# A planner that counts two more delays on early loads, and the issue order it was given anew

## Chip, core and metric

The kernel runs on one core of one Trainium2 chip. The metric is the device time of one execution in microseconds (us), lower is better. The kernel before takes 402.11 us, the median of 3 runs (401.63 to 402.58).

## What is computed

Eight batches (B=8) of eight heads (H=8), sequence S=576, head size D=64, 32 packing queries per head. Attention is done twice: the packing queries p attend to k and v, which gives 32 packed rows per head; then q attends to these packed rows, which serve as keys and as values. The heads side by side are x, the input of a gated convolution block.

```python
p_packed = softmax(p @ k.T / 8) @ v             # 32 rows per head
x        = softmax(q @ p_packed.T / 8) @ p_packed
h        = relu(x @ w_in)                       # 512 -> 1024
conv     = sum_k conv_w[k] * shift(h, k - 1)    # along the sequence
out      = (h * sigmoid(conv)) @ w_out          # 1024 -> 512
```

The weights w_in, conv_w and w_out arrive as 8-byte floats and are turned into 4-byte floats on the chip.

## The kernel before

Work is cut into 16 groups g of four heads (two groups per batch) and, behind them, 8 blocks j of 128 columns of the first product per batch and 36 tiles m of 128 rows of the second. Each group, batch and tile is a Python generator (a stream) whose steps name an engine, a duration, the events to wait for and the buffers to take.

Per group: k and q are loaded (L404, L415) and transposed, for the first four groups on PE (L444) with ScalarE copies behind (L450), later on VectorE (L427); p is scaled (L484) and transposed (L487); PE scores p against k (L460), VectorE takes the maximum (L515, `nm`), ScalarE the exponential (L519, `a`), PE transposes it (L547), ScalarE copies it (L550, `a1T`), PE multiplies by v (L557), ScalarE scales (L576, `pb`), PE transposes (L581), ScalarE copies (L584, `ppT`), PE scores against q (L460 again). Then VectorE does a softmax over the 32 packed rows (L591 to L615) with one ScalarE exponential inside (L601), and the result is split into a high and a low half (L619 `a2hi` on ScalarE, L621 `a2lo` on VectorE).

Per batch and half hf of the columns: PE multiplies the packed rows by w_in (L641), ScalarE and PE or VectorE split that (L656 `ghi`, L660, L664 `glo`). A block j of the first product is 12 matmuls at L705; ScalarE and VectorE apply relu, convolution and gate (L717, L721, L723, L727, L731, L733). The tiles of the second product are at L794; the last pairs use seven products in place of eight at L926. Weights are loaded in eight pieces (L305), narrowed by ScalarE (L275) and VectorE (L277, L282), and the w_out pieces are split with PE's help (L333, L338, L342).

What sets the order: a table of stream numbers, `ORDER`. `Flow.run` walks it, issues each stream's next step, and books the planned time of it with the costs of `Step` and `Flow`. So the order of instructions on each engine's queue comes from the table alone, and each engine works through its queue in that order. The planner's times have one effect on the program: while the first tile of the second product is not done, `fill` puts idle 128x128 matmuls (L251) in front of a PE step whose planned start leaves room, at 216 ns each. One such fill shows as two records in the profile.

All loads go through SyncE's queue (SP), with eight semaphores in turn: a ninth load waits until the first of the eight before it has landed. The planner's landing time of a load is the one before it in one chain of transfers plus its own duration.

Of the kernel before, what the change touches and what calls it, by code (L numbers as in the profile page):

```python
# [26 lines left out]
    "1a0u1n0m0u124f6e1n451l4d4e4f6e0u454f4d1a4h1c4e4e0u0u4f4g1b0y1k4d451b4i4f4f114j4i881n884k4i6e1g4h6f4j6e6e4i6f6e4k"
    "4h4k4i4j4i89161i121a4k4j4i6e1i6f6f121e1a4j4k4l891d126f6f6f6f4j4k4l1i6f1o4k6g121s4l1i4l6g4h124l8a4m1a4l6f1a1j4m1q"
    "191j1i1a6f4m4j121i6g1q8a1w6g6h6e4n6g4m6h1q204n1a1v6g1i6g4m1v4l1h6g4m1a4n124m121r1v4n6g6g236f8b1a6g4o121i4n1i4o4p"
    "6h6h4o4p4p1a236h124o8b4o6h4n1q6g4p1a6h6h6h4p6h4o1m4o1a1y4n234p4p1q1i6h1i1q4q282b1y4r6i1r1y6i1y1a1i6i126i6i1q1a2b"  # L30
    "4r6i12241a4q4q1z6i6j1a6i1a4r1i6i6i4s6i2b1p4s6j4s1q4t4u1q4s1i1y1i4t4s264t1t4t1q1z6k1y2g6j2c4u6j1y4u4s261i6j2j4u6j"
    "4s6k6j264u2j4v4t2j1q6j271i4u1u4v226i4u6j266j4t2e1x4w2k6j4t1i4v1q2e1i1q6k4w2e4v2a1i1q6h2f2e4v3p6k6k6k4w1y1i274x26"
    "6k1q6k6l1y4x6l216k6k6k2f4x1q6k4x2m1y4v50266m1q6l6l4w264v1q26262r2m6l2h4w6l2m2r506l4x2r6j6l4y4w2e1q2n2z4y4y2z1y1y"
    "2z374x1q296l2n2o6l6l6l4w4z4z1y1y4y4z516m4y6m6m6m6m6m1q4y6m6m504z4x4z514z4y524z256n6m526n536m52536n526n1y52535452"
    "536n54546n6n6n6n6n1y1y522w552m2e6o54556o1y266n2s51532u2e2u6n5a54376o6p5553556p1y552654546o3c305a1y6o6o6o6o372e2e"
    "6o6o2p1y6o265656566p6p266p6p532u556q6m26562u576p5556266p6p57566p3f576q56586p59266q6q576q6q58582d5957592m58583457"
    "58596q6q6q596o6q575859596r2e26322m5a6q6r26262e6s5b6r6r6r3226262m2e326s2m2m6r2i6p5b6r2e5c6r6r6q5b6r5c322e5d335c6r"
    "3f3f6s5c6s2v5c2u2e5c2v2e2e2e6s5e6t5c6t355f385d5d5d5d6s6s6s6s2l5f5f5e5e2e6s3a5e5d3a2m6s2m2u2m5k3a5f2m5d2u2q3b2u6t"
    "6u6u6t6r6t6t5f5e5k5f2m5g5f5e6t6t6t5k6t3g6t5h6u6u6u326u5h5h2t6s2m2m6u3a6v5h2m5h5e5h6u6u2x332u6u2m2e5h2y2e5i5j5g5g"
    "6t5i5g2m5i3i5j6v325i5j6u5l3i2u325l325i5j5j3b5g2u362m5i5i2m6v6v6v6v3a2u5j3i5g5j2u5g6v326v6v6v6v6v6w5m5m5l6w313i2u"  # L40
    "2u6x6x5n5n5o6w6w6w6w2u6w2u5n6w6w5o5m6u5m5o6w6w323j3a5m5o5o5n6x6x2u6x6x6y326x6x5n5o5o5m5n3i5m3a3a6x5n5p5p5q5p325q"
    "6x5r3d6y3e396x325p5p5q5q2u5q5p6y6y323a325p5r5r6y6y6y6y6y2u5s2u5q5q5t6y6z6x3j32325r5u325s6w32323a5t6z5r325t3i5s5t"
    "6y5r5v5s5t5s3i6z5s6z3i5r5s6z6z6z6z6z6z5t5u6y5t5u70706z3a3a5w5w703a707071828470705x5w3h5v715w5x70708070705y71715w"
    "83813a3a70715y5w855y5x5x7172835w5y725y5x713i717185715v715z5z72725z5z723a3a723i5z3a5z713i64725x73645y5z727272603i"
    "723i7386605x3i607473733a73723i6z615y607g60643i3i3a60607373733a6162747362627373636174637474747473623i636261636274"
    "3i6563613i63633i656162816175747466676587747466757j7h686666676766757575676867836675767575756766686775757j696a7k7k"
# [6 lines left out]
class Step:  # L53
# [131 lines left out]
def tile_packed_attention_conv_gate(  # L185
# [15 lines left out]
    HG = 4  # L201
# [307 lines left out]
    def attention(g):  # L509
# [44 lines left out]
        t = small()  # L554
# [514 lines left out]
```

## Time and profile before

| what | value |
|---|---|
| median of 3 runs | 402.11 us |
| profiled execution | 402.01 us, span 400.2 us, so 1.8 us lie outside the span |
| PE, VectorE, ScalarE busy | 392.2, 365.5, 284.1 us |
| PE clock granted | 1.00 of full speed in nearly every slice |
| DMA | 49.2 MB, 360 GB/s at 10 to 30 us |

PE is busy for 98% of the span, but some of this is the idle fills. VectorE is busy 91%, and idle in the main at the two ends. ScalarE is busy for 10.0 of 10 us in the stretches from 40 to 70 us and has room later. A row of the chain of waits gives a start, the time until the next piece begins, and what filled it.

### The profile page before, as it was taken

How to read it: one execution, taken by the hardware profiler on the slowest of the kernel's cores; microseconds unless marked ns; L12 is line 12 of the kernel's file. 1: busy time of each engine (PE TensorE's matmuls, PEld its weight loads, DVE VectorE, ACT ScalarE, POOL GpSimd, SP SyncE). 2: the span in 40 equal slices, each digit the busy share in tenths (PEclk: the TensorE clock that was granted, in tenths of full speed). 3: DMA queues.
4: the chain of work that ended last, by engine and by line, in shares of the span. 5: the costliest groups of instructions: out<-in, count | busy, mean ns of one | idle time of the engine just before them, and what ended most of it. 6: DMA issues, size and time to landing. Idle time of an engine off the chain costs nothing.

```text
span 400.2 us, 8463 instructions
## 1 busy us (share of the span) xinstructions
PE 392.2 (98%) x3393; PEld 318.8 (80%) x3393; DVE 365.5 (91%) x532; ACT 284.1 (71%) x497; POOL 1.6 (0%) x16
## 2 busy tenths in 40 slices
PE   7899999999999999999999999999999999999996
PEld 6668676778868877878869687878788787889996
DVE  0789999999999999999999999999999999999751
ACT  4989999977687588666765659738657678876440
POOL 1000000000000000000000000000000000000000
PEclk9999999999999999999999999999999999999999
DMA  8999999999858782966483539113600110001202
GB/s 304 357 361 267 276 264 163 128 156 146 121 94 112 122 196 68 156 88 153 79 153 79 97 100 157 48 51 97 122 2 27 52 41 19 23 2 52 78 28 79
DMA packets 140378, 49.19 MB, mean 123 GB/s; under 512 B 121244, under 2 KB 132788, under 8 KB 140340
## 3 DMA queue, kind: packets, MB, share of 16 engines
q1 hardware_dynamic: 140340, 48.67, 55.8%
q8 instruction: 26, 0.43, 0.5%
q14 instruction: 12, 0.10, 0.1%
HBM read 37.25 MB, written 9.44 MB: 117 GB/s over the span
## 4 chain that ended last, share of the span: by engine, by line
PE 84%; ACT 8%; DMA 5%; SPq 1%; issue 1%
PE fo L794 44%; PE big L705 23%; PE big L460 3%; PE big L641 3%; DMA q<-in_q_dram 3%; PE big L926 3%; DMA v<-in_v_dram 2%; PE sm L926 2%; PE sm L557 2%; ACT hgt L731 1%; ACT hgt L721 1%; PE big L547 1%; ACT hgt L275 1%; ACT glo L664 1%; SPq L404 1%; PE sm L794 1%
## 5 line engine op out<-in xcount | busy, mean ns | idle before, releaser
L794 PE MATMUL fo<-wo_hi,xhi 128*128 128x512 f32 x240 | 97.9, 408 | 0.0
L794 PE MATMUL fo<-wo_lo,xhi 128*128 128x512 f32 x240 | 94.8, 395 | 0.0
L794 PE MATMUL fo<-wo_hi,xlo 128*128 128x512 f32 x240 | 94.5, 394 | 0.0
L717 ACT ACTIVATE hbuf<-big 128x576 f32<-128x576 f32 x64 | 42.3, 668 | 30.1 <-PE big L705 29.5
L731 ACT ACTIVATE hgt<-hgt 128x576 f32<-128x576 f32 x64 | 43.9, 696 | 18.8 <-DVE hgt L727 18.6
L794 PEld LDWEIGHTS fo<-wo_hi,xhi 128*128 128x128 f32 x240 | 45.3, 189 | 13.3 <-issue 2.5
L705 PE MATMUL big<-a2hi,ghi 128*128 128x288 f32 x256 | 55.6, 298 | 0.1
L705 PE MATMUL big<-a2hi,glo 128*128 128x288 f32 x256 | 54.5, 294 | 0.0
L705 PE MATMUL big<-a2lo,ghi 128*128 128x288 f32 x256 | 54.3, 294 | 0.0
L794 PEld LDWEIGHTS fo<-wo_lo,xhi 128*128 128x128 f32 x240 | 45.1, 188 | 11.2
L723 DVE SCALAR_TENSOR_TENSOR hgt<-hbuf,cw,hgt 128x576 f32<-128x576 f32 x64 | 51.1, 802 | 2.5 <-ACT hgt L721 2.3
L794 PEld LDWEIGHTS fo<-wo_hi,xlo 128*128 128x128 f32 x240 | 45.1, 188 | 7.9
L727 DVE SCALAR_TENSOR_TENSOR hgt<-hbuf,cw,hgt 128x576 f32<-128x576 f32 x64 | 50.7, 803 | 0.4
L721 ACT ACTIVATE hgt<-hbuf,cw 128x576 f32<-128x576 f32 x64 | 50.3, 792 | 1.0
L733 DVE SCALAR_TENSOR_TENSOR hgt<-hgt,hbuf 128x576 f32<-128x576 f32 x64 | 47.1, 745 | 0.7 <-ACT hgt L731 0.4
L705 PEld LDWEIGHTS big<-a2hi,ghi 128*128 128x128 f32 x256 | 42.7, 188 | 5.1 <-ACT glo L664 1.0
L705 PEld LDWEIGHTS big<-a2lo,ghi 128*128 128x128 f32 x256 | 40.9, 188 | 0.0
L705 PEld LDWEIGHTS big<-a2hi,glo 128*128 128x128 f32 x256 | 40.9, 188 | 0.0
L747 DVE TENSOR_TENSOR xlo<-hgt,xhi 128x1024 fp32r<-128x1024 f32 (+1 forms) x36 | 35.8, 1002 | 0.0
L858 ACT COPY o<-fo 128x512 f32<-128x512 f32 (+1 forms) x32 | 18.5, 580 | 21.2 <-PE fo L794 19.6
L744 ACT CAST xhi<-hgt 128x1024 fp32r<-128x1024 f32 (+1 forms) x36 | 31.5, 881 | 2.2 <-DVE hgt L733 2.2
L515 DVE TENSOR_REDUCE nm<-big 128x1 f32<-128x576 f32 x16 | 11.9, 746 | 11.6 <-PE big L460 11.5
(191 smaller groups left out, 604.1 us busy)
## 6 DMA issues: line engine op xcount, KB each, us to landing
out_dram<-o SPq DMA_DIRECT2D x35, 256.0 KB, 3.3
v<-in_v_dram SPq DMA_DIRECT2D x16, 512.0 KB, 5.9
k<-in_k_dram SPq DMA_DIRECT2D x48, 144.0 KB, 4.2
q<-in_q_dram SPq DMA_DIRECT2D x48, 144.0 KB, 4.1
hgt<-in_moe_w_in_dram SPq DMA_DIRECT2D x3, 1024.0 KB, 11.2
hgt<-in_moe_w_out_dram SPq DMA_DIRECT2D x3, 1024.0 KB, 6.6
a1T<-stage SPq DMA_DIRECT2D x96, 20.0 KB, 1.8
hgt<-in_k_dram SPq DMA_DIRECT2D x2, 576.0 KB, 5.1
```

Of the source, the lines that this page charges most:

```text
L705: nc.tensor.matmul(out=t[:, hf, :SH], lhsT=w[:, gg, js], rhs=x[:, hf * SH : (hf + 1) * SH], start=n == 0, stop=n == 3 * NG - 1,)
L717: nc.scalar.activation(out=h[:, 1 : S + 1].rearrange("c (f s) -> c f s", f=2), in_=t[:, :, :SH], func=AF.Relu, scale=0.5)
L721: nc.scalar.activation(out=d, in_=h[:, 1 : S + 1], func=AF.Copy, scale=cw[:, NJ + j : NJ + j + 1])
L723: nc.vector.scalar_tensor_tensor(out=d, in0=h[:, 0:S], scalar=cw[:, j : j + 1], in1=d, op0=ALU.mult, op1=ALU.add)
L727: nc.vector.scalar_tensor_tensor(out=d, in0=h[:, 2 : S + 2], scalar=cw[:, 2 * NJ + j : 2 * NJ + j + 1], in1=d, op0=ALU.mult, op1=ALU.add)
L731: nc.scalar.activation(out=d, in_=d, func=AF.Tanh)
L733: nc.vector.scalar_tensor_tensor(out=d, in0=d, scalar=1.0, in1=h[:, 1 : S + 1], op0=ALU.add, op1=ALU.mult)
L744: nc.scalar.copy(out=hi[:, js, o], in_=src[:, js])
L747: nc.vector.tensor_tensor(out=lo[:, js, o], in0=src[:, js], in1=hi[:, js, o].bitcast(F32), op=ALU.subtract)
L794: nc.tensor.matmul(out=t[:, : fs.stop - fs.start], lhsT=x, rhs=w[:, c, fs], start=c + i == 0, stop=c == NJ - 1 and i == 2)
L858: nc.scalar.copy(out=o[:, fs], in_=sums_of[m, q][:, : fs.stop - fs.start])
L926: nc.tensor.matmul(out=turns[m, bank][:, at : at + 256], lhsT=x[:, c, :], rhs=y[:, c, :], start=first and c + i == 0, stop=c == 3 and i == ...
```

## The change

The planner is changed in how it books loads. A landing counts an added delay that depends on the time at which it falls (`LATE`: none before 16.5 us, 1.4 us up to 44 us, 2.4 us up to 62 us, 0.5 us after). Loads also have a size in a ring of 288 places (`ring`), and a load that finds no place in it waits for older ones to land. `LATER` goes from 620 to 640 ns. The figures for GpSimd's queue change too, but no step uses that queue. And the table `ORDER` is replaced by another. The steps, their operations and shapes, and the buffers are the same.

```diff
 ORDER = (
-    "0002043m0408043u0304030305060b3l0c06013k050b060c0g0c0c0b060605053q3v3k0e06070e070a3k063v06063k0j060e3v09060j3s0k"
...
+    "0004040402053m03043k030803050b060b0b0c0j0c0c0j06063k05063k3k0c3u0j05070e0601073k3k3v0606060r063v0g0e090k0e063v0f"
...
-    ISSUE = dict(SP=(465, 1100), POOL=(1050, 1000))
-    LATER, LANES = 620, 8
+    ISSUE = dict(SP=(465, 1100), POOL=(900, 1000))
+    LATER, LANES = 640, 8
     SLOW = ((4600, 1.28), (5500, 1.7))
+    LATE = ((16500, 0.0), (44000, 1400.0), (62000, 2400.0), (1e9, 500.0))
+    RING = 288
...
             if step.engine == "SP":
                 at = max(at, self.flights.pop(0))
+                while self.queued and (self.queued[0][0] <= at or sum(n for _, n in self.queued) + step.ring > self.RING):
+                    at = max(at, self.queued.pop(0)[0])
...
-        return at, self.data
+            if step.engine == "SP":
+                landed = self.data["SP"] = start + ns
+                self.flights.append(landed)
+                self.queued.append((landed, step.ring))
...
+        return at, landed + next(x for t, x in self.LATE if landed < t)
```

Lines of the changed kernel are 11 higher: L444 is L455 there, L251 is L262, L519 is L530. The first place is SP's queue, from the ninth load on. `hgt1` holds weight pieces, `hgt0` the q of the second group, `v_88` its v. Before:

```order
L404 DMA k_167<-in_k_dram 128x1152
L305 DMA hgt1_77<-in_moe_w_in_dram 128x2x1024
L404 DMA hgt0_76<-in_q_dram 128x1152
L388 DMA v_88<-in_v_dram 128x4x256
L392 DMA v_88<-in_v_dram 64x4x64
L305 DMA hgt1_77<-in_moe_w_in_dram 128x2x1024
L404 DMA k_284<-in_k_dram 128x1152
```

Now:

```order
L415 DMA k_250<-in_k_dram 128x1152
L399 DMA v_88<-in_v_dram 128x4x256
L403 DMA v_88<-in_v_dram 64x4x64
L415 DMA hgt0_76<-in_q_dram 128x1152
L316 DMA hgt1_77<-in_moe_w_in_dram 128x2x1024 x2
L415 DMA k_367<-in_k_dram 128x1152
```

The v and then the q of the second group now come ahead of both w_in pieces. The second place is ScalarE's queue around the exponential of the first group (`a1`), where `stage` is the first weight piece. Before:

```order
L450 COPY qT_128<-big_129 128x640
L519 ACTIVATE a1_163,sm1_164<-big_135,nm_154 128x576
L450 COPY kT_147<-big_148 128x640
L450 COPY kT_147<-big_169 128x512
L493 COPY pT_175<-sm_161 128x2x32 x2
L550 COPY a1T_187<-big_181 128x640
L450 COPY qT_128<-big_189 128x512
L275 ACTIVATE stage_70<-stage_70 128x1024
L275 ACTIVATE s2_158<-s2_158 24x128
L576 ACTIVATE pb_237<-sm_209,rs_230 128x128
```

Now:

```order
L504 COPY pT_150<-sm_148 128x2x32 x2
L495 ACTIVATE pm_160<-p_121 128x128
L461 COPY kT_153<-big_154 128x640
L530 ACTIVATE a1_172,sm1_173<-big_139,nm_170 128x576
L286 ACTIVATE s2_126<-s2_126 24x128
L461 COPY kT_153<-big_163 128x512
L506 COPY pT_193<-sm_168 128x128
L461 COPY qT_114<-big_178 128x512
L561 COPY a1T_207<-big_183 128x640
L368 COPY cw_72<-sm_212 128x24
L286 ACTIVATE stage_70<-stage_70 128x1024
L587 ACTIVATE pb_239<-sm_218,rs_196 128x128
```

The exponential stands behind the first copy of the second group's k, and the weight piece still stands ahead of `pb`. The third place is PE's queue from the transpose of the second group's exponential on. Before:

```order
L547 MATMUL big_289<-ident_64,a1_262 128x128 x5
L444 MATMUL big_298<-ident_64,k_167 128x128 x4
L251 MATMUL idle_311<-ident_64 128x128 x3
L444 MATMUL big_316<-ident_64,hgt0_76 128x128 x5
L355 MATMUL sm_323<-ident_64,cw_raw_71 128x24
L460 MATMUL big_327<-kT_273,pT_282 32x288 x8
L251 MATMUL idle_341<-ident_64 128x128
L444 MATMUL big_343<-ident_64,hgt0_76 128x128 x4
L557 MATMUL sm_350<-v_88,a1T_325 32x64 x20
```

Now:

```order
L558 MATMUL big_297<-ident_64,a1_263 128x128 x5
L262 MATMUL idle_303<-ident_64 128x128
L471 MATMUL big_305<-kT_256,pT_193 32x288 x8
L568 MATMUL sm_316<-v_88,a1T_314 32x64 x20
L262 MATMUL idle_342<-ident_64 128x128 x2
L455 MATMUL big_346<-ident_64,hgt0_76 128x128 x5
L592 MATMUL sm_359<-ident_64,pb_340 128x128
L455 MATMUL big_369<-ident_64,hgt0_76 128x128 x4
L262 MATMUL idle_381<-ident_64 128x128 x4
L471 MATMUL big_386<-qT_345,ppT_378 32x288 x8
L558 MATMUL big_395<-ident_64,a1_361 128x128 x5
L262 MATMUL idle_415<-ident_64 128x128 x12
L455 MATMUL big_429<-ident_64,k_367 128x128 x5
```

The transposes of q (`hgt0`) have moved behind the score of the third group (L471) and the product with v (L568), and a run of 12 fills now stands ahead of the k of the fourth group (`k_367`).

## Rows read from the trace of the kernel before

**Rows 1.** Busy time of each engine by stretch: length, then us (instructions)

```profile
0.00:10.00 10.00, 7.81 (x56) 6.80 (x57) 0.76 (x1) 4.20 (x9) 1.39 (x14) 1.00 0.82 304
10.00:20.00 10.00, 8.36 (x119) 6.38 (x119) 7.11 (x15) 9.07 (x21) 0.00 (x0) 1.00 1.06 358
20.00:30.00 10.00, 9.39 (x138) 6.74 (x138) 8.84 (x18) 8.12 (x21) 0.00 (x0) 1.00 1.06 360
60.00:70.00 10.00, 10.00 (x78) 6.84 (x66) 9.87 (x17) 10.00 (x18) 0.00 (x0) 1.00 1.21 163
100.00:150.00 50.00, 50.00 (x507) 39.31 (x506) 49.50 (x80) 35.68 (x68) 0.00 (x0) 1.00 0.77 128
350.00:400.20 50.20, 47.10 (x326) 43.63 (x324) 34.56 (x52) 24.17 (x46) 0.00 (x0) 0.99 0.13 48
```

**Rows 2.** Idle fills alone, one stretch and the sum: us (records)

```profile
40.00:50.00 10.00, 1.22 (x8) 1.14 (x8) 1.00 1.00 277
sum 400.00, PE 11.92 PEld 10.38; mean PE 1.32 PEld 1.15
```

**Rows 3.** Chain of waits, 30 to 80: start, us, what

```profile
34.07 1.02 ACT glo L664
36.05 1.07 ACT hgt L275
69.35 0.57 ACT hgt L731
71.64 0.92 ACT glo L664
72.61 5.05 PE big L705 x36
```

**Rows 4.** Who waited for whom, 0 to 60: us, times, longest

```profile
PE big L444 <- DMA hgt<-in_q_dram: 1.5, 1, 1.5
ACT pb L576 <- PE sm L557: 1.4, 1, 1.4
DVE hgt L277 <- DMA hgt<-in_moe_w_in_dram: 0.8, 1, 0.8
```

**Rows 5.** Two loads on SP: start, us

```profile
7.29 1.05 SPq L404 DMA_DIRECT2D hgt<-in_q_dram  x1
8.47 0.37 SPq L388 DMA_DIRECT2D v<-in_v_dram  x1
```

**Rows 6.** Time to landing of the first of these, by its line

```profile
DMA to landing us min/median/max: 12.5/12.5/12.5
```

**Rows 7.** Timeline, 9 to 35: start, us, engine, line, operation

```profile
9.76 0.74 ACT L519 ACTIVATE a<-big,nm 128x576 f32<-128x576 f32 x1 [0.80 <-DVE nm L515]
10.49 1.17 ACT L450 COPY kT<-big 128x640 f32<-128x640 f32 x2
12.81 1.27 ACT L275 ACTIVATE stage<-stage 128x1024 f32<-128x1024 f32 x1
14.08 0.34 ACT L576 ACTIVATE pb<-sm,rs 128x128 f32<-128x128 f32 x1
15.21 0.72 PE L460 MATMUL big<-qT,ppT 64*32 64x288 f32 x16
24.24 0.72 PE L460 MATMUL big<-qT,ppT 64*32 64x288 f32 x16
27.35 1.22 DVE L282 SCALAR_TENSOR_TENSOR w_in_sb<-hgt 128x1024 int32<-128x1024 int32 x1
...
33.45 1.73 PE L251 MATMUL idle<-ident 128*128 128x128 f32 x14
34.17 0.71 DVE L621 TENSOR_TENSOR a2lo<-a2t,a2hi 128x576 fp32r<-128x576 f32 x1
```

**Rows 8.** Chain of waits later: the same 16 matmuls twice

```profile
147.17 0.86 PE big L641 x16
158.04 1.02 PE big L641 x16
```

More of the change, by code (lines that the diff above doesn't have):

```diff
@@ L27 @@
[L27 to L46, printed above, removed]
@@ L50, with __init__ @@
+    "7w7c7a7u7u7v7x7a7e7a7a7a7x7z7s7x7y7a7e7v7x7y7a7y7a7d7v7f7d7z7a7x7z7z7a7d7d7d7d7d7d8c8c7d7d7d7d7d7d7d7d7d7d"
 )
 class Step:
-    def __init__(self, engine, ns, after=(), take=(), give=(), sets=None, cols=0, tiled=False, parts=1, loose=False):
+    def __init__(self, engine, ns, after=(), take=(), give=(), sets=None, cols=0, tiled=False, parts=1, loose=False, ring=8):
         self.engine, self.ns, self.after, self.take, self.give = engine, ns, after, take, give
-        self.sets, self.cols, self.tiled, self.parts, self.loose = sets, cols, tiled, parts, loose
+        self.sets, self.cols, self.tiled, self.parts, self.loose, self.ring = sets, cols, tiled, parts, loose, ring
@@ L90, in __init__ @@
         self.free = dict(PE=2500.0, ACT=1900.0, DVE=600.0, SP=580.0, POOL=1350.0)
-        self.data = 2700.0
+        self.data = dict(SP=2700.0, POOL=2700.0)
         self.issued = 0
         self.flights = [0.0] * 7
+        self.queued = []
         self.windows = {}
@@ L147, in transfers @@
                 at = max(at, self.flights.pop(0))
+                while self.queued and (self.queued[0][0] <= at or sum(n for _, n in self.queued) + step.ring > self.RING):
+                    at = max(at, self.queued.pop(0)[0])
             at += self.LATER if step.engine == "SP" and self.issued >= self.LANES else issue
             self.issued += step.engine == "SP"
-            slow = next((x for t, x in self.SLOW if self.data < t), 1.0)
-            self.data = max(self.data, at + delay) + step.ns / step.parts * slow
+            slow = next((x for t, x in self.SLOW if self.data["SP"] < t), 1.0)
+            ns = step.ns / step.parts * slow
+            start = max(self.data[step.engine], at + delay)
             if step.engine == "SP":
-                self.flights.append(self.data)
-        return at, self.data
+                landed = self.data["SP"] = start + ns
+                self.flights.append(landed)
+                self.queued.append((landed, step.ring))
+            else:
+                landed = self.data["POOL"] = start + min(max(0.0, self.data["SP"] - start), ns) + ns
+                self.data["SP"] = max(self.data["SP"], start) + ns
+        return at, landed + next(x for t, x in self.LATE if landed < t)
     def run(self, order):
@@ L301, in load_weight @@
         _, _, src, st = weight_tile(i)
-        yield Step("SP", 2500, after=[("wp", i - 3)] if i >= 3 else [], sets=[("wd", i)])
+        yield Step("SP", 2500, after=[("wp", i - 3)] if i >= 3 else [], sets=[("wd", i)], ring=16)
         if src.dtype != F32:
@@ L384, in load_v @@
         b, gg = divmod(g, NG)
-        yield Step("SP", 2250, take=["v"], sets=[("v", g)], parts=2)
+        yield Step("SP", 2250, take=["v"], sets=[("v", g)], parts=2, ring=24)
         t = grp[g]["v"] = vfree.pop(0)
@@ L408, in load_kq @@
             return
-        yield Step("SP", 4300, take=["kq"], sets=[(name, g)], parts=4)
+        yield Step("SP", 4300, take=["kq"], sets=[(name, g)], parts=4, ring=72)
         t = wk.tile([128, KQ], F32, name=name, tag="kq", bufs=3)
@@ L531, in attention @@
             nc.vector.transpose(out=moved[:, 4 - TAIL // 32 :, SV, :], in_=rest)
-            yield Step("SP", 1100, take=["a1T"], give=["ad"], parts=4 * HG)
+            yield Step("SP", 1100, take=["a1T"], give=["ad"], parts=4 * HG, ring=2)
             a1T = wk.tile([128, SV + 1, 128], F32, name="a1T", tag="a1T", bufs=1).rearrange("r s n -> r (s n)")
```

33 lines of the change are left out of this document (26 added, 7 removed).

## Prediction

> **What bounds the kernel now.** I read the busy time by stretch first. PE is busy for all of 60 to 70 us and of 100 to 150 us, and only the last stretch has some 3 us without work [rows 1]. ScalarE and VectorE tell the other half: in the first 30 us ScalarE is busy for 4.2, 9.1 and 8.1 us and VectorE for 0.8, 7.1 and 8.8 us; from 60 to 70 us ScalarE has no pause and VectorE 0.1 us; later ScalarE falls to 36 of 50 us [rows 1]. Part of PE's busy time is idle fills: 11.9 us of records, of which 1.2 us lie in the stretch from 40 us and none behind it [rows 2]. So there are three phases. Up to about 35 us loads and the chain of two groups feed ScalarE and VectorE badly. From there to the low 70s ScalarE is the bound. After that PE is.
>
> The chain of waits gives the two seams. At 34.07 us ScalarE begins the low half `glo` of the first packed weight, which lets the first block of the first product go on; from there on the chain runs mostly through ScalarE, one piece at its heels, until a third `glo` at 71.64 us releases PE's L705 at 72.61 us, and then PE runs without a break [rows 3]. From 72.6 us to the end of the span are 327.6 us, and 1.8 us lie outside it.
>
> **What the change can move.** It adds and removes no computing, only places in queues. Two counts of the new order against the old one carry the sum. First, the L705 at 72.61 us, the first block of the second batch, has exactly the same PE work ahead of it in both orders, but for 4 fills more (39 in place of 35). Second, ScalarE's instructions up to the one that releases it are the same but for one L731 less in the new order: there the last release is the `a1T` copy of the sixth group, which frees a buffer, since the third `glo` has moved forward. So the time is 72.6 us, shifted by how late ScalarE stands at about 35 us, less this L731, plus a remainder of PE work that stays.
>
> **Step 1, the remainder.** PE goes in and out of its tiled products (L460, L557, L641) 15 times after that L705 before, 14 times now. The 16 matmuls at L641 take 0.86 us to the next start where a tiled product follows and 1.02 us where L794 does [rows 8]: 0.16 us for leaving. Entering has no row of its own; it lies between nothing and as much again, and I take 0.09 us. One excursion less is -0.25 us.
>
> **Step 2, the L731.** One less, 0.57 us in the chain [rows 3]: -0.6 us.
>
> **Step 3, ScalarE at the first seam.** Up to the first `glo` the new queue holds one L275 less, a weight piece that before had gone ahead of it and now follows. A like piece takes 1.07 us in the chain [rows 3]. If `glo` ended at the same time, ScalarE would owe +1.1 us.
>
> **Step 4, when the first `glo` ends.** Before, that is 35.1 us. I walk the new queues with the durations of the rows.
> - The exponential of the first group ran at 9.76 us, the two copies of k at 10.49 us for 1.17 us [rows 7]. Now one copy stands ahead of the exponential, so it starts some 0.7 us later, the transpose behind it on PE too. The weight piece (1.27 us, 12.81 us before) still stands ahead of `pb` (14.08 us before) [rows 7], now behind a later `a1T`: `pb` at about 15.05 us. The score of the first group against q moves from 15.21 us [rows 7] to about 16.2 us. So the new order first loses 1.0 us.
> - Then it gains. Before, PE waited 1.5 us for the q of the second group [rows 4], a load issued at 7.29 us that took 12.5 us [rows 5, 6], and behind it in PE's queue stood the score of the third group and the second group's product with v. ScalarE stood 1.4 us waiting for that product, and VectorE 0.8 us for a w_in piece [rows 4]. Now v and q of the second group are issued ahead of both w_in pieces and the transposes of q stand behind the product. At 358 GB/s [rows 1], q has 0.46 MB less ahead of it (a piece of 1.05 MB less, v's 0.59 MB more) and would land 1.3 us sooner, near 18.5 us in place of 19.8 us; v, issued at 8.47 us before [rows 5], has the piece and q's 0.59 MB less ahead of it, 4.6 us. The product with v then waits only for ScalarE's copy, and the second group's score against q starts at about 22.75 us in place of 24.24 us [rows 7]: -1.5 us.
> - It gives part back. Between the second group's maximum and its sum VectorE had one conversion of 1.22 us (L282) [rows 7]; now two stand there, and one narrowing ahead. So the sum, which followed at once, comes no sooner than before but 0.3 us later. Two items then move behind the second group's `a2lo` (34.17 us before [rows 7]), so this starts near 33.5 us.
> - ScalarE's `glo` follows at 33.6 to 34.5 us in this walk, so it ends 0.6 us sooner than before.
>
> The walk's own error is about 1 us. Its bounds: the early 1.0 us is not made up at all, so `glo` ends 1.0 us later; or the 1.5 us carries through, and it ends 1.5 us sooner.
>
> The 12 fills in a row are 2.8 us by the run of seven that took 1.73 us [rows 7]. They begin near 24.1 us and end near 26.9 us. What they stand before, the k of the fourth group, should land near 26 us: behind q come two w pieces and k, 2.7 MB or 7.5 us, after 18.5 us. So they cost about 1 us of PE that has nothing else queued, and ScalarE is busy with `a1T` until 27.2 us anyway; I book 0.4 us, inside the walk.
>
> The Trainium skill (DMA: Bandwidth & Descriptors, Latency and other measured facts) speaks against a delay set by the clock: it gives memory access as 0.2 us on average and 2 us at high load, so where the queue is empty the planner's 1.4 us would be too much. Here the loads in question run at 358 to 360 GB/s [rows 1], high load by any reading, and by that the added delay fits. At light load k would land 1.2 us sooner, an estimate from the planner's 1.4 us less the page's 0.2 us, and the sum below would keep its 0.4 us as pure loss.
>
> **Sum.** -0.6 (step 4) + 1.1 (step 3) - 0.6 (step 2) - 0.25 (step 1) = -0.35 us on 402.01 us, the profiled execution, which stands 0.1 us under the median of 402.11 us. I predict 401.7 us. With the bounds of step 4 alone it is 400.8 to 403.3 us.
>
> **Rivals.**
> - *The recovered waits carry through.* PE, ScalarE and VectorE each drop their wait of 0.8 to 1.5 us [rows 4], the second group's score comes 1.5 us sooner and the two conversions fall into pauses. `glo` ends at 33.6 us or sooner, and with fewer pauses on VectorE at the seam up to 1 us more is gained: 402.0 - 1.5 + 1.1 - 0.6 - 0.25 = 400.8, down to 399.8; I take 400.2 us. For it: all three waits go back to loads that the new order issues sooner or asks for later. Against it: the early loss of 1.0 us.
> - *The early loss stays (the other side).* ScalarE is the mechanism, its place the queue between 10 and 24 us: the exponential behind the copy of k, the weight piece ahead of `pb`, and then the copies of the third group, two of q and the exponential of the third group ahead of the second group's `ppT`. If `ppT` comes no sooner than before, so that the score stays at 24.24 us [rows 7] or later, nothing is recovered: +1.0 + 1.1 - 0.6 - 0.25 = 403.3 us, and with the 12 fills holding PE for another 0.5 us 403.8 us. VectorE would owe 1.5 us then as well, two items moved behind `a2lo`. For it: ScalarE has no pause from 60 to 70 us in which to catch up [rows 1].
> - *The start is hidden.* PE could be the bound from the first seam on, since it has the same work to do; then only fills and excursions count, 4 x 0.25 - 0.25 us: 402.8 us. Against it: the chain runs through ScalarE there [rows 3].
>
> **Chances.** The forecast has 0.36 (400.9 to 402.5 us), the recovered waits 0.31, the early loss 0.28, the hidden start 0.05. A measurement of this kernel tells about 0.2%, or 0.8 us, from no change, so 401.3 to 402.9 us is the same. Faster: 0.31 and a quarter of the forecast, 0.40. Slower: 0.28, and 0.05 from the upper ends, 0.33. Same: 0.27. Cases of both signs hold most of the chance, so the range is wide, 399.3 to 404.6 us: the rivals' times, with an unmodelled 0.8 us on either side.
>
> **What would show it.** In the profile of the changed kernel: no wait of PE's transposes for the q of the second group, and none of `pb` for L557 over 0.5 us; the exponential of the first group near 10.5 us and the score of the first group near 16.2 us; that of the second group near 22.75 us; the first `glo` ending near 34.5 us; the first L705 of the second batch at about 72.5 us (72.6 - 0.6 + 1.1 - 0.6), released by ScalarE; from there to the end 327.3 us. I am wrong if the L705 is released by PE or VectorE, if new pauses on PE of more than 0.5 us stand after 80 us, or if the last 50 us, where PE already lacks 3 us of work [rows 1], change by more than 0.5 us.

## The result, and the profile after

The changed kernel takes 404.82 us in the median (403.19 to 405.61, 6 runs), the kernel before beside it 402.37 us. The ratio is 1.0051, 95% interval 1.0031 to 1.0071: slower, by 2.1 us, where I had forecast 0.4 us less. The profiled execution took 404.57 us with a span of 402.5 us.

PE is TensorE; in the rows DVE is VectorE, ACT is ScalarE and POOL is GpSimd. The view by stretch, as in [rows 1]: length, then busy us of PE, PE's weight load, VectorE, ScalarE, GpSimd (instructions), then the granted clock, the DMA share and GB/s. Two stretches of 10 us are new; behind them they stand as the kernel before has them.

```profile
10.00:20.00 10.00, 9.57 (x169) 6.52 (x168) 7.10 (x14) 9.21 (x24) 0.00 (x0) 1.00 1.06 372
20.00:30.00 10.00, 10.00 (x122) 8.13 (x123) 9.68 (x18) 8.80 (x18) 0.00 (x0) 1.00 1.05 378
60.00:70.00 10.00, 10.00 (x58) 6.72 (x42) 10.00 (x17) 10.00 (x17) 0.00 (x0) 1.00 0.98 202
100.00:150.00 50.00, 49.86 (x434) 38.94 (x434) 48.67 (x74) 36.17 (x66) 0.00 (x0) 1.00 0.63 131
190.00:200.00 10.00, 9.19 (x50) 7.82 (x50) 8.91 (x17) 5.08 (x9) 0.00 (x0) 1.00 0.77 190
240.00:250.00 10.00, 8.94 (x100) 7.32 (x99) 8.96 (x14) 6.77 (x12) 0.00 (x0) 1.00 0.74 178
350.00:402.50 52.50, 48.84 (x341) 45.35 (x339) 35.84 (x54) 27.77 (x53) 0.00 (x0) 1.00 0.14 51
```

```profile
190.00:200.00 10.00, 10.00 (x60) 8.91 (x59) 9.93 (x15) 8.11 (x13) 0.00 (x0) 1.00 0.46 77
240.00:250.00 10.00, 10.00 (x130) 7.50 (x129) 9.85 (x16) 9.16 (x17) 0.00 (x0) 1.00 1.00 162
```

The start is better: PE is busy for 9.57 and 10.00 us of the second and third stretch, where it had 8.36 and 9.39 [rows 1]. Part of this is idle fills, 6.93 us now and 5.64 us before; without them PE does 12.6 us of work in these 20 us where it did 12.1. The loss stands where the forecast had looked for nothing: 0.81 us of PE without work between 190 and 200 us, 1.06 us between 240 and 250 us. Before, PE had no pause from 80 us to 350 us.

PE's wait for the q of the second group, ScalarE's for the product behind it and VectorE's for the w_in piece [rows 4] are gone. The fills' records, one stretch and the sum against [rows 2], us (records):

```profile
20.00:30.00 10.00, 4.29 (x34) 4.03 (x34) 1.00 1.05 378
sum 400.00, PE 12.79 PEld 10.99; mean PE 12.79 PEld 10.99
```

The run of 12 lies there. The timeline of the start, line by line against [rows 7]: start, us, engine, line, operation.

```profile
10.21 0.75 ACT L530 ACTIVATE a<-big,nm 128x576 f32<-128x576 f32 x1
13.96 0.37 ACT L587 ACTIVATE pb<-sm,rs 128x128 f32<-128x128 f32 x1
15.18 0.71 PE L471 MATMUL big<-qT,ppT 64*32 64x288 f32 x16
21.94 0.72 PE L471 MATMUL big<-qT,ppT 64*32 64x288 f32 x16
32.03 1.02 ACT L675 CAST glo<-big 128x1024 fp32r<-128x1024 f32 x1
71.37 0.53 PE L716 MATMUL big<-a2hi,ghi 128*128 128x288 f32 x2
```

The first score against q stands where it stood (15.18, before 15.21 us), that of the second group comes 2.3 us sooner, the first `glo` ends at 33.05 us (before 35.09), and the first block of the second batch starts at 71.37 us in place of 72.61 [rows 3]: 1.24 us won. From there to the end of the span it was 327.6 us, and now is 402.5 - 71.37 = 331.1 us: 3.5 us lost.

The chain of waits shows where. First around 180 to 197 us, then around 236 to 243 us: start, us, what (SPq is SyncE issuing DMAs).

```profile
192.90 4.03 DMA out_dram<-o
197.00 0.59 ACT o L869
...
197.64 5.87 PE fo L805 x24
...
236.17 0.59 SPq L548
...
236.81 5.75 DMA v<-in_v_dram
...
242.69 1.17 PE sm L568 x40
```

Before, the chain ran through PE alone here. The SP queue of the changed kernel in these stretches (start, us, operation, count):

```profile
176.17 0.36 SPq L871 DMA_DIRECT2D out_dram<-o  x1
...
180.53 10.27 SPq L548 DMA_DIRECT2D a1T<-stage  x16
...
192.90 0.60 SPq L871 DMA_DIRECT2D out_dram<-o  x1
...
225.72 11.04 SPq L548 DMA_DIRECT2D a1T<-stage  x16
236.81 1.85 SPq L399 DMA_DIRECT2D v<-in_v_dram  x1
```

The last six groups (10 to 15) rearrange their exponential with 16 DMAs within the chip (L548), and issuing these takes 10.27 and 11.04 us in the two rows shown. At 192.90 us a store follows them whose tile ScalarE had written by 176.15 us (L869 at 175.57 us, 0.58 us). There are two `o` buffers, so the second copy after that waits for its landing:

```profile
197.00 0.59 ACT L869 COPY o<-fo 128x512 f32<-128x512 f32 x1 [2.33 <-DMA out_dram<-o]
197.64 0.51 PE L805 MATMUL fo<-wo_hi,xhi 128*128 128x512 f32 x1 [0.81 <-ACT o L869]
```

And the v of group 13 lands when PE has stood waiting for it for 1.06 us. The PE queue after, then the same product and its v load in the kernel before:

```profile
240.91 0.72 PE L471 MATMUL big<-qT,ppT 64*32 64x288 f32 x16
242.69 1.17 PE L568 MATMUL sm<-v,a1T 128*32 128x64 f32 x40 [1.06 <-DMA v<-in_v_dram]
243.79 0.52 PE L716 MATMUL big<-a2hi,ghi 128*128 128x288 f32 x2
```

```profile
236.69 0.43 SPq L388 DMA_DIRECT2D v<-in_v_dram  x1
244.18 0.71 PE L460 MATMUL big<-kT,pT 64*32 64x288 f32 x16
244.83 0.77 PE L557 MATMUL sm<-v,a1T 128*32 128x64 f32 x40
245.52 1.09 PE L641 MATMUL big<-w_in_sb,ppT 64*32 64x512 f32 x16
```

The load is issued at the same time in both (236.69 and 236.81 us) and lands near 242.6 us in both. Before, the product stood at 244.83 us, 2.3 us behind the landing; the new order puts it two blocks of L716 sooner. From the score to what follows the product it is 1.34 us before and 2.88 us after: 1.5 us lost. At 197 us it is 1.0 us (the last L716 starts at 196.42 us and takes 0.26 us to the next start). Of 3.5 us some 1.0 us are left, and PE's time without work accounts for them. Between 70 and 150 us it stands for 0.27 us at 81.50 us and 0.14 us between 110 and 120 us. From 350 us to the end of the span it lacks 3.66 us of work where it lacked 3.10, 0.56 us more. There the last copy of an output tile waits for a store to land, where before it waited for PE (the changed kernel, then the kernel before):

```profile
399.39 0.37 ACT L869 COPY o<-fo 128x256 f32<-128x256 f32 x1 [1.92 <-DMA out_dram<-o]
```

```profile
397.14 0.37 ACT L858 COPY o<-fo 128x256 f32<-128x256 f32 x1 [2.35 <-PE fo L794]
```

### The profile page after: what moved, and what is told of

It reads as the page before. It is cut to its first block, busy times and chain, and to the rows that moved or that the text cites. A ratio compares the mean times of both kernels' runs of the same rounds, so it can differ in the third digit from the quotient of the medians.

```text
span 402.5 us, 8477 instructions
## 1 busy us (share of the span) xinstructions
PE 393.4 (98%) x3401; PEld 319.2 (79%) x3401; DVE 365.4 (91%) x532; ACT 284.0 (71%) x497; POOL 2.1 (1%) x16
## 4 chain that ended last, share of the span: by engine, by line
PE 64%; ACT 10%; DVE 10%; SPq 7%; DMA 6%; issue 2%; DVEq 0%; ACTq 0%
PE fo L805 33%; PE big L716 18%; SPq L548 5%; PE big L471 3%; DMA out_dram<-o 3%; PE big L937 2%; PE big L652 2%; PE sm L937 2%; PE sm L568 2%; DMA v<-in_v_dram 1%; DMA p<-in_p_dram 1%; SPq L426 1%; DVE hgt L734 1%; DVE hgt L738 1%; ACT hgt L732 1%
## 5 line engine op out<-in xcount | busy, mean ns | idle before, releaser
L805 PE MATMUL fo<-wo_hi,xhi 128*128 128x512 f32 (+1 forms) x244 | 99.0, 406 | 0.8 <-ACT o L869 0.8
L805 PE MATMUL fo<-wo_lo,xhi 128*128 128x512 f32 (+1 forms) x244 | 95.9, 393 | 0.0
L805 PE MATMUL fo<-wo_hi,xlo 128*128 128x512 f32 (+1 forms) x244 | 95.8, 393 | 0.0
L742 ACT ACTIVATE hgt<-hgt 128x576 f32<-128x576 f32 x64 | 43.6, 688 | 24.9 <-DVE hgt L738 24.9
L805 PEld LDWEIGHTS fo<-wo_hi,xhi 128*128 128x128 f32 x244 | 46.1, 189 | 14.5 <-issue 4.4
L734 DVE SCALAR_TENSOR_TENSOR hgt<-hbuf,cw,hgt 128x576 f32<-128x576 f32 x64 | 51.7, 810 | 4.8 <-ACT hgt L732 4.5
L716 PE MATMUL big<-a2hi,ghi 128*128 128x288 f32 x256 | 55.1, 297 | 0.1
L805 PEld LDWEIGHTS fo<-wo_lo,xhi 128*128 128x128 f32 x244 | 45.8, 188 | 11.0
L716 PE MATMUL big<-a2hi,glo 128*128 128x288 f32 x256 | 54.3, 294 | 0.0
L716 PE MATMUL big<-a2lo,ghi 128*128 128x288 f32 x256 | 54.2, 293 | 0.0
L805 PEld LDWEIGHTS fo<-wo_hi,xlo 128*128 128x128 f32 x244 | 45.9, 188 | 8.1
L738 DVE SCALAR_TENSOR_TENSOR hgt<-hbuf,cw,hgt 128x576 f32<-128x576 f32 x64 | 51.4, 808 | 0.6
L716 PEld LDWEIGHTS big<-a2hi,ghi 128*128 128x128 f32 x256 | 42.9, 188 | 5.7 <-ACT glo L675 1.1
L716 PEld LDWEIGHTS big<-a2hi,glo 128*128 128x128 f32 x256 | 40.9, 188 | 0.0
L716 PEld LDWEIGHTS big<-a2lo,ghi 128*128 128x128 f32 x256 | 40.9, 188 | 0.0
L869 ACT COPY o<-fo 128x512 f32<-128x512 f32 (+1 forms) x32 | 18.4, 576 | 26.3 <-PE fo L805 18.2
```

Of the source, the lines that this page charges most:

```text
L716: nc.tensor.matmul(out=t[:, hf, :SH], lhsT=w[:, gg, js], rhs=x[:, hf * SH : (hf + 1) * SH], start=n == 0, stop=n == 3 * NG - 1,)
L734: nc.vector.scalar_tensor_tensor(out=d, in0=h[:, 0:S], scalar=cw[:, j : j + 1], in1=d, op0=ALU.mult, op1=ALU.add)
L738: nc.vector.scalar_tensor_tensor(out=d, in0=h[:, 2 : S + 2], scalar=cw[:, 2 * NJ + j : 2 * NJ + j + 1], in1=d, op0=ALU.mult, op1=ALU.add)
L742: nc.scalar.activation(out=d, in_=d, func=AF.Tanh)
L805: nc.tensor.matmul(out=t[:, : fs.stop - fs.start], lhsT=x, rhs=w[:, c, fs], start=c + i == 0, stop=c == NJ - 1 and i == 2)
L869: nc.scalar.copy(out=o[:, fs], in_=sums_of[m, q][:, : fs.stop - fs.start])
```

## The experiments

**Theory A**: the new order asks PE for some data about as soon as their load can land, at a few places; SP's queue, full of a1T copies, puts the landing late, and the loss is there. **Theory B**: VectorE sets the pace behind 70 us, and the pauses only show slack. **Theory C**: SP is late as a whole, and a wait that is removed comes back at the next load. **Theory D**: the head of the new order is itself the loss. **Rival E** concerns the clock: idle fills hold the granted clock at its upper level, so leaving them out costs what it saves. Ratios are against the kernel before on the same chip; its median was 402.5 to 402.8 us there.

**store_first.** One line moved on SP, all other queues unchanged.

```diff
+L871 DMA out_dram<-o 128x512
 L548 DMA a1T<-stage 32x160 x16
 L399 DMA v<-in_v_dram 128x4x256
 L403 DMA v<-in_v_dram 64x4x64
-L871 DMA out_dram<-o 128x512
```

> Against the changed kernel (404.82 us, 1.0051 of the kernel before) one place on SP's queue is moved and nothing else on any engine: the store of an output tile whose copy was ready at 176.15 us, and which stood behind the 16 a1T copies of group 11 until 192.90 us, now stands ahead of them. Theory A (SP's queue is the cause: a store and a v load stand behind a1T copies that take 10.3 to 11.0 us to issue, and PE's two new pauses of 0.8 and 1.1 us with their re-entry are those): ScalarE's copy to o at 197.00 us waits for no landing, PE's L805 at 197.64 us starts about 1.1 us sooner, and the time falls by 1.1 us to 403.7 us, ratio 1.0033. Theory B (VectorE, which ends most waits of ScalarE behind 60 us, sets the pace, and the two pauses on PE only show slack that it leaves): PE stands for a product of ScalarE or VectorE a little later instead; 404.4 to 404.8 us.

Measured: 406.54 us (403.41 to 410.31), ratio 1.0076 [1.0047, 1.0104]. Not shorter, as theory A had it; that it is longer than the changed kernel isn't settled, since the intervals overlap. The profiled execution is the one of 410.31 us, so its rows tell what happened there, not what makes the median. Its stretch from 240 to 250 us, and PE's two waits for a v:

```profile
240.00:250.00 10.00, 6.89 (x81) 5.61 (x80) 8.28 (x12) 2.82 (x5) 0.00 (x0) 0.83 0.68 168
62.74 0.77 PE L568 MATMUL sm<-v,a1T 128*32 128x64 f32 x40 [2.04 <-DMA v<-in_v_dram]
246.91 1.70 PE L568 MATMUL sm<-v,a1T 128*32 128x64 f32 x40 [3.11 <-DMA v<-in_v_dram]
```

The pause at 197 us is gone, and that for the v of group 13 has grown from 1.1 to 3.1 us. But the edit touches nothing ahead of 176 us, and this execution was late before: at 62.74 us PE had stood 2.0 us for the v of group 4. The v of group 13 is issued at 242.44 us, 5.6 us later than in the changed kernel's profile, and PE reaches its place only 2.2 us later. Without the first pause PE comes some 1.0 us sooner against SP, so the first may have shortened the second; that would be theory C for this one pair, and it is argued, not shown. The granted clock is 0.83 in that stretch: part of it at the lower of the two levels, 1.2 GHz, after PE had stood. Of the nine other executions the four longest (406.83 to 408.59 us) have a mean granted clock of 0.992 to 0.996, the five others (403.41 to 406.25 us) one of 0.998 or more. The Trainium skill (TensorE: Matmul & The Clock Gate, Part 1: The HAM clock gate) has it that the throttled state is the default and activity lifts it; by that a pause costs more than its length, and the trace agrees: behind the pause of 3.1 us the product takes 1.63 us to the next start, behind that of 1.06 us, at a clock of 1.00, 1.10 us.

**v_first, both_first.** The v of group 13 ahead of the a1T copies; then this and the store.

```diff
 L871 DMA out_dram<-o 128x512
-L548 DMA a1T<-stage 32x160 x16
 L399 DMA v<-in_v_dram 128x4x256
 L403 DMA v<-in_v_dram 64x4x64
+L548 DMA a1T<-stage 32x160 x16
```

> Again one place on SP's queue: the two loads of group 13's v, issued at 236.81 us behind the 16 a1T copies of that group, now stand ahead of them (near 225.7 us; the buffer is free since PE's L568 of group 11 at 204.6 us). The a1T copies come 1.1 us later. Theory A: PE's L568 no longer waits for v (1.06 us of pause, 1.5 us of lost PE time in the stretch from 240 to 250 us), the time falls by 1.5 us to 403.3 us, ratio 1.0023. Theory C (SP is full there, so the wait only changes its name): L568 waits for the last a1T copy instead, which lands near 240 to 242 us; 403.9 to 404.8 us. Theory B: 404.4 to 404.8 us.

> Both moves on SP's queue together. Theory A: 1.1 + 1.5 = 2.6 us, so 402.2 us, ratio 0.9996: the change would then have been worth nothing to 0.3 us, with these two places as its whole loss. Theory B: 404 us or more, because what PE does not lose to SP it loses to VectorE. Theory C: 403.5 us.

Measured: v_first 403.30 us, 1.0022 [1.0011, 1.0033]; both_first 403.62 us, 1.0018 [1.0001, 1.0034]. In v_first's stretch PE is full again, and its waits behind 60 us name no v:

```profile
240.00:250.00 10.00, 10.00 (x105) 8.28 (x104) 10.00 (x16) 7.20 (x14) 0.00 (x0) 1.00 0.60 127
```

The v alone gave what theory A said, 1.2 us by the ratios and 1.5 by the medians; the interval of v_first just overlaps that of the changed kernel. The expectation had one thing wrong: the buffer is not free from 204.6 us on, because the v of group 14, loaded at 193 us, holds it; v could move by only the a1T copies. With both moves the median was not 402.2 but 403.6 us, while the profiled executions (402.36 and 402.44 us) were the lowest or second lowest of twelve, up to 405.0 us. So some places cost time in some executions and not in others. Even the pause for the store all but goes without a move of the store: PE is busy for 9.87 us between 190 and 200 us in v_first's profiled execution. Between landing and use I then found, in the changed kernel, 1.2 us for the v of group 4 (issued at 50.02 us) and 0.9 us for the v of group 7 (issued at 105.02 us, used at 112.50), while the v of group 8 was issued at 100.77 us and used at 123 us. For group 7 that is new: before, its v landed at 64.7 us and was used at 112.33 us. For group 4 it isn't. In the kernel before, the second part of its v took 7.3 us from issue to landing, and the product stood 0.3 us behind that:

```profile
51.86 0.61 SPq L392 DMA_DIRECT2D v<-in_v_dram  x1
59.48 0.77 PE L557 MATMUL sm<-v,a1T 128*32 128x64 f32 x40
```

At group 4 PE does wait in some executions: of the nine profiled kernels with the new order there, five show it, for 0.3 to 2.0 us, and four don't. None shows a wait for the v of group 7.

**product_late.** No load moved; PE's product of group 13 behind a block of L716 and a piece of L805.

```diff
 L471 MATMUL big<-qT,ppT 32x288 x8
-L568 MATMUL sm<-v,a1T 32x64 x20
 L716 MATMUL big<-a2hi,ghi 128x288 x2
...
 L805 MATMUL fo<-wo_lo,xhi 128x512
+L568 MATMUL sm<-v,a1T 32x64 x20
```

> The changed kernel with no load moved: PE's product of group 13 with v (L568, 242.69 us, which waited 1.06 us for v) stands behind one more block of L716 and one piece of L805, 2.3 us of work that was behind it. Theory A (the new order asks for this v about 4 us sooner against its load than the old one: before, the load was issued at 236.69 us and used at 244.83 us, 2.3 us after it landed): the pause of PE goes as it does when the load is moved, 404.8 - 1.5 + 0.25 (an excursion more into tiled products) = 403.5 us, ratio 1.002. Theory C (SP's queue as a whole runs late and the next wait takes its place): 404.3 to 404.8 us, with PE waiting for another landing behind 245 us. The kernel with v moved forward gave 1.0022 [1.0011, 1.0033].

Measured: 403.35 us, 1.0016 [1.0000, 1.0031]. This product, at 243.72 us, no longer waits; the one wait for a v that is left is that of group 4:

```profile
59.51 0.77 PE L568 MATMUL sm<-v,a1T 128*32 128x64 f32 x40 [0.32 <-DMA v<-in_v_dram]
243.72 0.77 PE L568 MATMUL sm<-v,a1T 128*32 128x64 f32 x40
```

Moving the use does what moving the load did. For group 13 it was the distance between the two, not the load.

**loads_first, v_loads.** In loads_first both moves, the v of group 4 ahead of the k of group 5, and the v of groups 7 and 8 in each other's place (the rows read alike). In v_loads the store and the a1T copies stand as in the changed kernel; the v of groups 4, 7 and 8 move as in loads_first, and the v of groups 13 and 14 change places too.

```diff
 L316 DMA hgt_77<-in_moe_w_out_dram 128x2x1024
+L399 DMA v<-in_v_dram 128x4x256
+L403 DMA v<-in_v_dram 64x4x64
 L426 DMA k<-in_k_dram 32x36x32 x4
 L316 DMA hgt_77<-in_moe_w_out_dram 128x2x1024
-L399 DMA v<-in_v_dram 128x4x256
-L403 DMA v<-in_v_dram 64x4x64
```

> Four loads or stores of the changed kernel moved forward on SP: the store and the v of group 13 as in the last kernel of the study that had both, and the v of group 4 (issued at 49.87 us, landed at 57.78 us, used at 58.96 us) ahead of the k of group 5, and the v of group 7 (used 0.95 us after landing) changes places with that of group 8, which lay there for 17.8 us. Theory A (places with 1 us between landing and use cost time in those executions where a load lands later; the median of 403.6 us against 402.4 us of the profiled execution comes from such places): the median falls to 402.4 to 402.9 us, ratio 0.9985 to 1.001, and the runs lie closer together than 402.4 to 405.0 us. Theory B (VectorE is what is late): 403.4 to 403.8 us, as with two moves.

> The changed kernel with its v loads alone moved: those of groups 13 and 14, and of groups 7 and 8, in each other's place, and that of group 4 ahead of the k of group 5. The store stays behind the a1T copies, the 12 fills stay. Theory A (the time between a v's landing and its use is the loss): 1.0051 - 0.0029 (v of group 13) - 0.0017 (the others) = 1.0005, 402.8 us; the pause of PE for the store near 197 us, 0.8 us, may be left, and then 1.0015. Theory C (SP's queue is late as a whole): 1.0035 or more, with PE waiting for another landing.

Measured: loads_first 402.31 us, 1.0001 [0.9988, 1.0014]; v_loads 402.36 us (401.95 to 403.00), 0.9993 [0.9982, 1.0003]. Moving v loads alone takes back the whole loss, and the runs lie within 1.1 us. It doesn't follow that the change lost all of it at these places: the v of group 4 was as close before. Waits on PE in the profiled executions, loads_first (404.21 us) and v_loads:

```profile
PE sm L568 <- DMA a1T<-stage: 1.0, 3, 0.4
```

```profile
PE fo L805 <- ACT o L869: 0.7, 1, 0.7
```

In loads_first's profiled execution theory C shows: the v of group 13 stands ahead of its a1T copies, which begin at 230.18 us (225.72 in the changed kernel), and the product waits for these instead. Exchanging two v loads puts nothing ahead of the copies. The pause for the store is still in v_loads; what it costs was not shown by itself. How much of the step from 1.0022 to 0.9993 is the v of group 4 and how much that of group 7 was not tried.

**old_product_early.** The close place made in the kernel before: the product ahead of two blocks of L705.

```diff
+L557 MATMUL sm<-v,a1T 32x64 x20
 L705 MATMUL big<-a2hi,ghi 128x288 x2
...
 L460 MATMUL big<-kT,pT 32x288 x8
-L557 MATMUL sm<-v,a1T 32x64 x20
```

> The kernel before, with one move on PE and nothing else: the product of group 13 with v (L557 at 244.83 us) ahead of two blocks of L705, where the new order has it against its load. It would stand at 240.97 us, and the v lands at 242.56 us. Theory A: PE pauses 1.6 to 1.8 us for v, and pays 0.25 us for one excursion more: 402.0 + 1.9 = 403.9 to 404.3 us by its own execution, ratio 1.0045. Theory B (such pauses only show slack that VectorE leaves on PE): ratio 1.001 or less.

Measured: 404.02 us (402.86 to 405.84), 1.0037 [1.0021, 1.0052], near theory A. Its profiled execution doesn't show the pause. It had lost time at the start already (2.5 us for a q, a wait of 1.5 us before [rows 4]), so the product came at 242.21 us, as its v landed (issued at 237.49 us, 4.5 us to landing), and has no wait:

```profile
PE big L444 <- DMA hgt<-in_q_dram: 2.5, 1, 2.5
242.21 0.97 PE L557 MATMUL sm<-v,a1T 128*32 128x64 f32 x40
```

The sign is shown by eleven timings and the place by the edit; the pause itself is not shown.

**old_order_new_plan, new_order_old_plan.** The two halves of the change apart; only the fills differ.

```diff
-    LATER, LANES = 620, 8
+    LATER, LANES = 640, 8
...
+    LATE = ((16500, 0.0), (44000, 1400.0), (62000, 2400.0), (1e9, 500.0))
```

> The planner's half of the change alone: the old order under the planner that counts the added delays. Its only effect is on idle fills: 9 in place of 3 in one run, one more run of 1 elsewhere, 41 in all in place of 35. Theory A: the added fills stand ahead of work that waits for a load, and hold it back by up to 1 us: 402.4 to 403.4 us, ratio 1.000 to 1.0025. If the planner's half were the loss, as a rival to the order, it would be 404 us or more.

> The other half: the new order under the old planner. Again only fills differ, 8 ahead of the fourth group's k in place of 12, 37 in all in place of 39. Theory A (the order holds the loss, by its loads, and the four fills fewer give back 0.3 to 0.9 us): 404.0 to 404.6 us, ratio 1.003 to 1.0045. If the planner's half were the loss: 402.4 us or less.

Measured: 402.92 us, 0.9999 [0.9982, 1.0017], and 404.65 us (402.19 to 407.43), 1.0059 [1.0035, 1.0083]. The loss belongs to the order. It hasn't become less under the old planner. It isn't in every execution either: the profiled one of new_order_old_plan took 402.19 us, and there the v of group 13 landed at 240.9 us, just as PE came to its product at 240.92 us.

**no_long_fill, all_first2, few_fills, six_fills.** The fills. no_long_fill is both_first without the run of 12; all_first2 has the store moved, the v loads as in v_loads, and no run of 12; few_fills drops the runs of 2 to 4 as well; six_fills is all_first2 with 6 of the 12.

```diff
-            self.warm(n)
+            n == 12 or self.warm(n)
```

> The kernel with both moves (403.6 us, ratio 1.0018), and the 12 idle fills ahead of the transposes of the fourth group's k are left out; every other instruction stands where it stood. The k landed at 24.80 us and the transposes began at 25.96 us. Theory A (PE has nothing else to do there, and the fills only hold back k by 1.1 us): transposes near 25.0 us, and what follows at the first seam is up to 1.1 us sooner; ScalarE is behind it by then, so 0.4 us of it is left: 403.2 us, ratio 1.001. Rival E (the fills keep the granted clock at 1.00; without them it falls to its lower level for the products behind): granted clock under 1.00 between 20 and 30 us and 404 us or more.

> The new order with what the runs so far have shown to cost: the store ahead of the a1T copies of group 11, the v of groups 13 and 14 in each other's place on SP (so that the v of group 13, used at 242.54 us, is loaded at 193 us and that of group 14, used at 260.20 us, at 237 us, and no a1T copy comes later), the v of groups 7 and 8 likewise, the v of group 4 ahead of the k of group 5, and the 12 idle fills left out. Theory A with the sizes measured apart: the two places 1.0051 to 1.0018, the other v loads 1.0018 to 1.0001, the fills another 0.0030: ratio 0.997, 401.3 us, faster than both kernels. Theory B (VectorE is late in any case, and what is won at the start is spent by 130 us): not under 402.2 us.

> The same, and also the six other runs of 2, 3 and 4 idle fills left out (16 matmuls, 3.5 us); the first run of 5 and the single ones stay. Theory A (PE's queue is held back wherever a fill still runs when the data land, by up to 0.2 us a run): 0.2 to 0.6 us less than with these fills, 400.8 to 401.2 us. Rival E (the clock): granted clock under 1.00 in a stretch between 5 and 50 us, and 402 us or more.

> The kernel with everything moved (ratio 0.9986), with 6 of the 12 idle fills kept: they end near 24.6 us, where the fourth group's k lands at 24.8 to 25.4 us. Theory A with the clock (without the 12 fills the granted clock was 0.66 between 25 and 30 us in the profiled execution, and four of twelve executions, the ones with a mean of 0.996 or less, took 402.3 to 403.1 us, the others 401.2 to 403.0 us): the clock stays at 1.00, the k is not held back, 401.3 us, ratio 0.997. If six fills hold k back as twelve do: 402.0 to 402.4 us. If they don't hold the clock: as with none, 402.0 us with the same spread.

Measured: no_long_fill 402.18 us, 0.9988 [0.9977, 1.0000]; all_first2 402.00 us, 0.9986 [0.9974, 0.9998]; few_fills 402.29 us, 1.0000 [0.9984, 1.0017]; six_fills 401.62 us (401.15 to 403.73), 0.9984 [0.9971, 0.9998]. The stretch from 25 to 30 us in no_long_fill, all_first2, few_fills and six_fills, one fence each:

```profile
25.00:30.00 5.00, 4.55 (x82) 3.25 (x86) 4.93 (x8) 4.89 (x11) 0.00 (x0) 1.00 1.09 345
```

```profile
25.00:30.00 5.00, 4.25 (x29) 4.12 (x37) 4.93 (x9) 3.95 (x8) 0.00 (x0) 0.66 1.08 342
```

```profile
25.00:30.00 5.00, 3.95 (x28) 3.39 (x31) 4.93 (x8) 4.07 (x8) 0.00 (x0) 0.70 1.07 351
```

```profile
25.00:30.00 5.00, 4.71 (x89) 3.35 (x93) 4.93 (x9) 4.91 (x11) 0.00 (x0) 1.00 1.08 339
```

Theory A on the fills and rival E both hold. Without the 12, PE waits about 2 us for k and starts on it at once. The gain against both_first is 1.2 us by the ratios, three times what I expected, and the two intervals lie just apart. Against v_loads, which keeps the 12, all_first2 gains 0.3 us, the store's move included, and those intervals overlap. So the cost of the 12 lies between 0.3 and 1.2 us and is not settled. But in all_first2 the granted clock fell in some executions: of its twelve, three had a mean of 0.996 or less (402.25, 402.43 and 403.14 us; the expectation of six_fills wrongly says four), the other nine a median of 401.67 us. no_long_fill had three as well (402.43 to 403.15 us), though its profiled execution shows 1.00. few_fills had eleven at 0.996 or less, its fastest of 401.66 us among them, so a lower mean alone doesn't tell the time. Six fills held it: no run of six_fills is below 0.999. six_fills is 0.16% faster than the kernel before, though its interval doesn't set it apart from all_first2, and it stays short of the 0.997 that the single sizes add up to.

**new_head, late_splice.** Two splices: the new order for its first 278 or 740 steps, then the old order for the rest.

```diff
-ORDER = new
+ORDER = new[:278] + [the steps of old that these leave, in old's order]
```

> The new order for its first 278 steps (to PE's work of about 62 us), then all other steps in the old order; the planner is the new one. The first seam and the first block of the second batch should be as in the changed kernel (first glo at 32.0 us, L716 of the second batch near 71.4 us, 1.2 us sooner than before), and behind them no a1T copy stands where the new order puts it. Theory A: the head keeps its 1.2 us and the tail loses nothing: 401.2 us, ratio 0.997. Theory B (the gain of the head is spent at once, since VectorE is as late as before by 80 us and PE waits for it between 70 and 120 us): 402.0 to 402.6 us. Theory D (the head itself is the loss, since it leaves VectorE more to do at 60 us): 403 us or more.

> The new order for its first 740 steps (PE's work to about 176 us, ahead of the store and the v that cost time), then the old order for all that is left. At 170 us PE of the changed kernel was 0.9 us of useful work ahead of the kernel before. Theory A: this is kept, 401.5 to 402.0 us, ratio 0.998. Theory B: the changed kernel has spent its gain by 130 us (0.3 us ahead there), and 402.3 to 402.8 us is what is left. A new wait at the splice, as in the first splice (PE for the v of group 4), would give 403 us or more; then the splice says nothing.

Measured: 402.57 us, 0.9996 [0.9986, 1.0006], and 405.28 us, 1.0071 [1.0055, 1.0088]. PE's two longest waits behind 60 us in new_head and in late_splice:

```profile
PE sm L568 <- DMA v<-in_v_dram: 1.1, 1, 1.1
PE big L716 <- ACT glo L675: 1.0, 1, 1.0
```

```profile
PE sm L592 <- ACT pT L506: 1.2, 1, 1.2
PE fo L805 <- ACT o L869: 0.7, 1, 0.7
```

The first is again the v of group 4, at 60.41 us, where the new order still holds; the other three stand behind the splices, and the changed kernel doesn't have them there. So neither tells A from B. new_head speaks against theory D: with the new head and without the new tail nothing is lost.

## Why the prediction was wrong, step by step

**Step 4, the first `glo`**, was right in its mechanism and too small: 33.05 us in place of 34.5. The early loss of 1.0 us did not come. The exponential ran at 10.21 us, 0.45 us later and not 0.7. And I had set the weight piece behind a later `a1T` without taking out the copy of q (0.64 us) that stood between them before and now stands ahead of `a1T`; so `pb` ran at 13.96 us, not 15.05, and the score at 15.18 us, not 16.2. The gain of 1.5 us at the second group's score was 2.3 us. For the start that is the first rival, "the recovered waits carry through", which had 0.31; its time of 400.2 us did not come.

**Steps 2 and 3**, one L731 less and one L275 owed, came out in size: from the end of `glo` to the L716 of the second batch I had 38.0 us, and it was 38.3. But no wait for ScalarE stands in front of it: the transpose of `pm` (L498) and the products of L652 run right up to it, and PE is busy for all of 60 to 70 us. That is one of the signs I had named for being wrong.

**Step 1 is the step that failed**: "a remainder of PE work that stays". I had counted the excursions (-0.25 us) and taken the rest of PE's 327 us as work alone, because PE ran there without a break before. It became 331.1 us, where the forecast had 327.3. Of the 3.5 us more than before, the place of the v of group 13 is 1.5 us, the place behind the store 1.0 us, the end of the span 0.56 us and small pauses 0.4 us, all in the one profiled execution; runs confirm the first of these (1.2 us by v_first, 1.4 us by product_late, in ratios), and the others rest on the trace alone. The new order moves uses against loads over the whole table, not only at the start, and I had compared loads and uses only up to 35 us. For the v of group 13 the two queues show it without a run: on SP its load stands behind the same 16 a1T copies in both, and on PE its product stands two blocks sooner. New pauses on PE of more than 0.5 us after 80 us, which I had named as a sign of being wrong, are what came. So did the third sign, by a little: the last 50 us lack 0.56 us more.

**The 12 fills** were booked at 0.4 us. They hold PE about 1.0 us past the landing of k (near 24.9 us, 12.3 us after its issue; its transposes start at 25.96 us), the size the walk had. How much of that reaches the end was 1.2 us by one pair of runs and 0.3 us by another, so whether 0.4 us was too little stays open.

**The delay in the planner** I had left as it was, on the ground of the loaded queue. The planner's half alone did nothing (ratio 0.9999); whether the delay has the right size no run shows, and the 12 fills that overrun the landing of k by 1.0 us rather speak for a smaller one. No rival had a wait in the steady stretch; all three were about the first 35 us. The sign of the slower rival was right by accident.

## What to carry to other kernels

When an order is replaced, take each load in both orders, from the first to the last, and set the time from its landing to its use beside what stands ahead of it on its queue; where that falls to about 1 us or less, the place can cost time in some executions and not in others, so one profile doesn't tell. Look at the old order's places too: the v of group 4 had 0.3 us in the kernel before. A stretch in which the bound engine never paused says how much work it has, not that it won't pause when its order changes. Where two loads stand in the wrong order of their uses, exchange them: it moves no other work, whereas a load moved ahead of the a1T copies made PE wait for these in one profiled execution (loads_first).

## What was not expected of the hardware

- Issuing counted here: 16 DMAs of 20 KB kept SP for 10.1 to 11.2 us in both kernels, some 0.6 us each, and what stood behind them was late. The Trainium skill (DMA: Bandwidth & Descriptors, Issuing engines are not separate DMA queues) calls the time to start a DMA usually small beside the DMA itself; for these copies, 1.8 us in the median from issue to landing, the trace shows a queue of a full 10 us of it.
- Idle fills work both ways: 12 of them cost 0.3 to 1.2 us. With none the granted clock fell to 0.66 between 25 and 30 us in one profiled execution (all_first2, after PE had stood 2.1 us) and stayed at 1.00 in another (no_long_fill, after 2.0 us). With 6 no execution fell below a mean of 0.999.
- A pause of 3.1 us on PE came with a granted clock of 0.83 over the 10 us around it; the pauses of 0.8 and 1.1 us left it at 1.00.
